# First unit's gates loaded on their own in sixteen rows, and another order of loads, scans and copies ahead of the first score

## The chip, the cores and the metric

The kernel runs on one core of a Trainium2 chip. The metric is the device time of one execution in microseconds (us). Before the change its median over three runs is 1085.26 us (1085.22 to 1085.31). The core's engines work side by side, each through its own queue in program order, and wait for each other on semaphores: TensorE (PE: matmuls and transposes; PEld is its weight load), VectorE (DVE), ScalarE (ACT), GpSimd (POOL), and SyncE (SP), whose queue issues the transfers (DMA).

## The reference

Attention with a forget gate, then two expert layers. Only the attention matters here, and in it the gate `f`:

```python
scores = scale * np.matmul(q, k.transpose(0, 1, 3, 2))     # q, k: (2, 8, 576, 64)
log_f = np.log(np.clip(f, 0.0001, 1.0))                     # f: (2, 8, 576)
cum = np.cumsum(log_f, axis=-1)
decay = cum[:, :, :, None] - cum[:, :, None, :]
scores = np.where(causal, -1000000000.0, scores + decay)
...                                                         # softmax over the keys, times v
x = attn_out.transpose(0, 2, 1, 3).reshape(B * S, H * D)    # then both expert layers on x
```

So the score of query i and key j needs the running sum of log f at i and at j.

## The kernel before, in words

The work is one long program. Attention comes first (to about 205 us of the span), then the expert layers. In attention the queries of each batch are cut into tiles of 128 rows; a unit is one tile and two heads. A loop over half units (one head at a time) issues for each: the exponential of the half unit before, two score matmuls, some warm-up matmuls into an unused PSUM tile (`warm`), transposes and value matmuls of earlier units, and a piece of the preparation of the next tile.

fp32 operands are split in a high and a low part (`hl`: ACT casts the high part, DVE subtracts to get the low part), transposed on PE into PSUM (`pt`), and copied out ("evacuated") into `qa`, `qb` for the queries and `kt`, `kb` for the keys. A score takes two matmuls: `qa` by `kt`, then `qb` by `kb`. The tiles `qb` and `kb` carry, in their rows from 64 up, constants and the running sums of log f, so that the second matmul adds the decay as well. `f` is loaded as 16 rows (2 batches by 8 heads) of 576; it is clamped, its log is taken, a scan makes the running sum `cum`, and `chl` holds the high and the low part of `cum`. For tile 0 (the first 128 positions) four transfers put these rows into `kb` and `qb` directly from `chl`. For all other tiles `chl` is written to DRAM (`cd`) and read back from there (`cum_k`, `cum_q`).

Nothing is reordered by a scheduler: each engine runs its instructions in the order in which the code issues them. The change touches the stretch from the first load to the first score, and the first step of the loop:

- L100: the activation table is loaded first on ACT.
- L199 to L209: loads of `f`, of the first 128 rows of q and k by halves of the heads (`raw`), and of the next 128 rows (`early`), all on SP.
- L211 to L217: constants; the clamp of `f`; the identity `idr` for the transposes.
- L219 to L249 (`cumulate`): log, scan, high and low part of `cum`, and the transfers from them. It is called for the positions 0 to 128 (L249), and for 128 to 576 in two parts.
- L253 to L266: mask and constant rows, written by GpSimd (`k_rows` is L190).
- L686 on: the splits of tile 0's first heads (L354, L355), 12 warm-ups, the transposes (L361) and evacuations (L307 to L313) of the first four heads, 8 warm-ups, the loop. The list `first` holds what the first two steps of the loop do for the other four heads. In the same steps the loop splits tile 1's `early` rows into `big` (L317, L319, L321) and transposes them.

The evacuations are shared out by `pick`, which gives each to ACT or DVE by a running estimate of how long each is busy.

## Time and profile before

| | |
|---|---|
| median of three runs | 1085.26 us |
| the profiled execution | 1085.22 us |
| its span, first to last instruction | 1083.4 us |
| outside the span | 1.8 us |
| PE busy | 1076.9 us, 99% of the span |
| DVE busy | 840.0 us, 78% |
| ACT busy | 545.0 us, 50% |
| POOL busy | 57.0 us, 5% |

Times in a profile count from the start of the span. In a timeline a row is: start, duration, engine, line of the kernel, operation, what is written and read, the shape, the number of instructions merged into the row, and in brackets how long the engine had been idle before and who released it. An fp32 matmul of the program is two passes on PE and shows as two. Instructions of one engine overlap a little at their ends, so the distance from start to start is shorter than the duration. SPq rows are the queue that issues transfers; the row ends when the transfer is issued, not when it lands. The view of windows gives busy time, and the number of instructions, of each stretch; PEclk there is the granted TensorE clock as a share of full speed.

### The profile page before, as it was taken

Reading aid. Unit: us, or ns where it says so; the run is one execution under the profiler, and the core shown is the slowest. Engines: PE = TensorE matmul, PEld = TensorE weight load, DVE = VectorE, ACT = ScalarE, POOL = GpSimd, SP = SyncE. Lnnn points to the kernel's source line nnn. Section 1 sums busy time; section 2 is a strip of 40 time slices with the busy share of each in tenths; the row PEclk is TensorE's granted clock in tenths of the full one; section 3 lists DMA queues with packets and bytes.
Section 4 is the critical chain, followed back from the end, with each engine's and each line's share of the span. In section 5 each row is a group of like instructions: output and inputs, shape, how many; then the busy total and the mean of one; then the engine's idle time right before and its main releaser. Section 6 shows DMA issues by size and latency. Waiting matters only on the chain.

```text
span 1083.4 us, 18373 instructions
## 1 busy us (share of the span) xinstructions
PE 1076.9 (99%) x6844; PEld 963.7 (89%) x6844; DVE 840.0 (78%) x1897; ACT 545.0 (50%) x1295; POOL 57.0 (5%) x110
## 2 busy tenths in 40 slices
PE   9999999999999999999999999999999999999998
PEld 8787779998989899898988989899898989899997
DVE  7856647878797888977888787887976559788994
ACT  7867632454426243343524435253442458787881
POOL 6422310000000000000000000000000000000000
PEclk9999999999999999999999999999999999999999
DMA  6534202023241424425343342524322341161402
GB/s 147 153 82 114 65 21 78 1 98 114 92 146 63 148 83 146 136 89 156 110 144 106 109 147 98 160 84 146 127 95 81 128 155 43 64 205 59 166 1 88
DMA packets 103805, 114.98 MB, mean 106 GB/s; under 512 B 35236, under 2 KB 63860, under 8 KB 103716
## 3 DMA queue, kind: packets, MB, share of 16 engines
q1 hardware_dynamic: 103716, 113.81, 33.2%
q8 instruction: 54, 0.88, 0.3%
q14 instruction: 35, 0.29, 0.1%
HBM read 82.24 MB, written 27.07 MB: 101 GB/s over the span
## 4 chain that ended last, share of the span: by engine, by line
PE 97%; DVE 1%; ACT 0%; issue 0%; POOL 0%; DVEq 0%; ACTq 0%; POOLq 0%
PE bank L858 33%; PE bank L1268 29%; PE bank L1740 9%; PE bank L1650 4%; PE ph L828 3%; PE x L568 3%; PE spare L1650 2%; PE bank L1579 2%; PE pa L858 2%; PE pa L641 2%; PE ph L622 1%; PE sp L468 1%; PE pt L532 1%; PE pt L361 1%; PE wt L395 1%; PE sp L469 1%
## 5 line engine op out<-in xcount | busy, mean ns | idle before, releaser
L858 PE MATMUL bank<-w2h,big 128*128 128x512 f32 x924 | 296.7, 390 | 0.0
L858 PE MATMUL bank<-w2l,big 128*128 128x512 f32 x528 | 205.7, 390 | 0.0
L858 PEld LDWEIGHTS bank<-w2h,big 128*128 128x128 f32 x924 | 173.4, 188 | 36.1 <-DVE hid_b L836 0.2
L1297 ACT COPY snap<-bank 128x288 f32<-128x288 f32 x168 | 66.8, 397 | 167.6 <-PE bank L1268 165.4
L835 ACT ACTIVATE big<-c 128x288 fp32r<-128x288 f32 x168 | 74.8, 445 | 84.7 <-DVE c L1302 81.3
L858 PEld LDWEIGHTS bank<-w2l,big 128*128 128x128 f32 x528 | 99.1, 188 | 20.0
L836 DVE SCALAR_TENSOR_TENSOR big<-c,big 128x288 fp32r<-128x288 f32 x140 | 64.0, 457 | 56.6 <-ACT big L835 53.9
L1033 DVE SCALAR_TENSOR_TENSOR acc<-bank,P,acc 128x512 f32<-128x512 f32 x132 | 92.2, 744 | 14.9 <-PE bank L858 14.8
L1268 PE MATMUL bank<-tt,ss 128*128 128x288 f32 x672 | 102.8, 295 | 0.0
L1268 PE MATMUL bank<-xh,ss 128*128 128x288 f32 x448 | 102.7, 295 | 0.0
L1268 PEld LDWEIGHTS bank<-tt,ss 128*128 128x128 f32 x672 | 93.1, 188 | 0.1
L1302 DVE TENSOR_TENSOR c<-bank,snap 128x288 f32<-128x288 f32 x168 | 75.7, 450 | 18.8 <-PE bank L1268 18.6
L1014 ACT CAST hb<-da 128x512 fp32r<-128x512 f32 x38 | 23.7, 623 | 106.8 <-DVE da L989 95.9
L1268 PEld LDWEIGHTS bank<-xh,ss 128*128 128x128 f32 x448 | 76.3, 188 | 0.0
L1268 PE MATMUL bank<-xl,ss 128*128 128x288 f32 x224 | 66.1, 295 | 0.0
L1268 PE MATMUL bank<-xh,w1l 128*128 128x288 f32 x224 | 66.0, 295 | 0.0
L1268 PE MATMUL bank<-xl,w1h 128*128 128x288 f32 x224 | 65.9, 294 | 0.0
L1268 PE MATMUL bank<-xh,w1h 128*128 128x288 f32 x224 | 65.7, 293 | 0.0
L858 PE MATMUL bank<-w2h,hid_b 128*128 128x512 f32 x132 | 51.4, 389 | 0.0
L75 DVE TENSOR_TENSOR w2l<-stg,w2h 128x512 fp32r<-128x512 f32 x60 | 41.2, 689 | 13.0 <-ACT w2h L74 12.9
L512 POOL TENSOR_SCALAR p<-p,rs 128x256 f32<-128x256 f32 (+5 forms) x72 | 41.8, 592 | 91.2 <-DVE rs L508 52.2
L1268 PE MATMUL bank<-tt,w1h 128*128 128x288 f32 x224 | 46.0, 293 | 0.0
(313 smaller groups left out, 2446.3 us busy)
## 6 DMA issues: line engine op xcount, KB each, us to landing
stg<-in_moe_w_dram SPq DMA_DIRECT2D x64, 512.0 KB
wb<-w_in_b SPq DMA_DIRECT2D x42, 256.0 KB
raw<-in_moe_w_in_dram SPq DMA_DIRECT2D x16, 512.0 KB
raw<-in_moe_w_out_dram SPq DMA_DIRECT2D x16, 512.0 KB
w_in_b<-hb SPq DMA_DIRECT2D x18, 256.0 KB
w_out_h<-hb SPq DMA_DIRECT2D x16, 256.0 KB
w_out_l<-da SPq DMA_DIRECT2D x16, 256.0 KB
w_in_f<-da SPq DMA_DIRECT2D x12, 256.0 KB
```

Source lines behind the costliest of these rows:

```text
L75: (lo_engine or nc.vector).tensor_tensor(out=lo, in0=raw, in1=f(hi), op=ALU.subtract)
L512: nc.gpsimd.tensor_scalar(out=p[:n, a, :nk], in0=p[:n, a, :nk], scalar1=r[:n, a:a + 1], scalar2=1.0, op0=ALU.mult, op1=ALU.mult,)
L568: nc.tensor.matmul(out=x[64 * a:64 * a + 64, h // 2, :n], lhsT=vts[b, j][:w, h + a, :], rhs=pT[:w, 128 * j + 64 * a:128 * j + 64 * a + 64] ...
L835: nc.scalar.activation(out=hh, in_=ph, func=AF.Relu)
L836: nc.vector.scalar_tensor_tensor(out=hl, in0=ph, scalar=0.0, in1=f(hh), op0=ALU.max, op1=ALU.subtract)
L858: nc.tensor.matmul(out=pa, lhsT=a_[:, ts_], rhs=w[wn][ft_], start=(first and n == 0), stop=(last and n == 2),)
L1033: nc.vector.scalar_tensor_tensor(out=acc[t], in0=pa, scalar=P[:, t, e:e + 1], in1=acc[t], op0=ALU.mult, op1=ALU.add)
L1268: nc.tensor.matmul(out=by_chunk(out_) if len(v_.shape) == 3 else out_, lhsT=u, rhs=v_, start=first and m == 0, stop=m == 5, skip_group_che ...
L1297: nc.scalar.copy(out=t, in_=bank["x", g])
L1302: nc.vector.tensor_tensor(out=t, in0=bank[of, g], in1=snap[with_, g], op=ALU.add)
L1650: nc.tensor.matmul(out=out_, lhsT=a_(kk, pa), rhs=b_(kk, pb), start=first and q == 0, stop=q == 5, skip_group_check=True,)
L1740: nc.tensor.matmul(out=bk[b][:, cs], lhsT=a_[:, ts_], rhs=w[wn][i][:, cs], start=i == 0 and q == 0, stop=i == 3 and q == 2,)
```

## The change

1. The gates of the first unit (batch 0, positions 0 to 128) are loaded on their own into `fe`, in sixteen rows: heads 0 to 3 twice, then heads 4 to 7 twice. Heads 0 to 3 come by SP's queue, heads 4 to 7 by ACT's; the activation table is loaded behind ACT's. DVE clamps `fe`, ACT takes the log, DVE scans it, and two DVE instructions turn each pair of copies into high and low part, in place by row: `part` and `sign`, made from the identity, are 0, 1 or -1 by row, so that a row becomes either the high part or what is left of it. One transfer per operand and half of the heads then fills both rows, four in all; the second two follow the loads of `early`.
2. The load of all of `f` comes behind the first halves of q and k. Its clamp runs on GpSimd ahead of the mask. Its log is taken in one piece (576 wide); the scan is cut at 256, one part before and one behind the evacuations of the first heads; high part (ACT) and low part (DVE) are made in one piece of 576, the low part behind the first score's reduction. The two direct transfers to `qb[1]` that followed `cd` are gone.
3. Of the first four heads ACT evacuates both query tiles and DVE both key tiles, instead of by `pick`; two of the 8 warm-ups stand between the query and the key transposes.

```diff
-    nc.scalar.preload_act_table_set("natural_log_exp_and_others")
...
                 out=t[:, 4 * g:4 * g + 4], in_=src[0, 4 * g:4 * g + 4, 0:128, :].rearrange("h p d -> p h d")
             )
 
-        nc.sync.dma_start(out=ft, in_=fg.rearrange("b h s -> (b h) s"))
+        fe, ce, me, he = (acc[0][:16, 128 * i:128 * i + 128] for i in range(4))
+        for g, queue in enumerate((nc.sync, nc.scalar)):
+            queue.dma_start(
+                out=fe[8 * g:8 * g + 8],
+                in_=fg[0, 4 * g:4 * g + 4, :128].unsqueeze(0).to_broadcast([2, 4, 128]),
+            )
+        nc.scalar.preload_act_table_set("natural_log_exp_and_others")
         for nm in "qk":
             raws[nm, 0, 0] = rawp.tile([128, H, D], F32, tag="raw", name="raw")
         for g in range(2):
             load_half(raws["q", 0, 0], q, g)
             load_half(raws["k", 0, 0], k, g)
+            if g == 0:
+                nc.sync.dma_start(out=ft, in_=fg.rearrange("b h s -> (b h) s"))
 
         early = stage.tile([128, 2, H, D], F32, tag="stg", name="early")
-        for a, (nm, src) in enumerate((("q", q), ("k", k))):
-            nc.sync.dma_start(out=early[:, a], in_=src[0, :, 128:256, :].rearrange("h p d -> p h d"))
-            raws[nm, 0, 128] = early[:, a]
+
+        def load_early():
+            for a, (nm, src) in enumerate((("q", q), ("k", k))):
+                nc.sync.dma_start(out=early[:, a], in_=src[0, :, 128:256, :].rearrange("h p d -> p h d"))
+                raws[nm, 0, 128] = early[:, a]
 
         nc.vector.memset(zer, 0.0)
         make_identity(nc, idn)
         k_rows(256, 384, nc.vector)
         q_rows(0, nc.gpsimd)
         q_rows(1, nc.gpsimd)
-        nc.vector.tensor_scalar(out=ft, in0=ft, scalar1=1e-4, scalar2=1.0, op0=ALU.max, op1=ALU.min)
+        nc.gpsimd.tensor_scalar(out=ft, in0=ft, scalar1=1e-4, scalar2=1.0, op0=ALU.max, op1=ALU.min)
+        part = acc[1][:16, :2]
+        sign = acc[1][:16, 8:9]
+        nc.vector.tensor_reduce(
+            out=part, in_=idn[:16, :16].rearrange("p (g a h) -> p a g h", g=2, a=2), axis=AX.XY, op=ALU.add
+        )
+        nc.vector.tensor_tensor(out=sign, in0=part[:, 0:1], in1=part[:, 1:2], op=ALU.subtract)
         nc.vector.tensor_copy(out=idr, in_=idn)
-
-        def cumulate(lo, hi, part=None):
-            w = hi - lo
-            if part != 1:
-                cumulate_a(lo, hi, w)
-            if part != 0:
-                cumulate_b(lo, hi)
-
-        def cumulate_a(lo, hi, w):
-            nc.scalar.activation(out=ft[:, lo:hi], in_=ft[:, lo:hi], func=AF.Ln)
+        nc.vector.tensor_scalar(out=fe, in0=fe, scalar1=1e-4, scalar2=1.0, op0=ALU.max, op1=ALU.min)
+        nc.scalar.activation(out=fe, in_=fe, func=AF.Ln)
+
+        def scan(o, i, init):
             nc.vector.tensor_tensor_scan(
-                out=cum[:, lo:hi], data0=ft[:, lo:hi], data1=zer.to_broadcast([16, w]),
-                initial=cum[:, lo - 1:lo] if lo else 0.0, op0=ALU.add, op1=ALU.add,
+                out=o, data0=i, data1=zer.to_broadcast([16, i.shape[1]]), initial=init, op0=ALU.add, op1=ALU.add,
             )
 
-        def cumulate_b(lo, hi):
-            nc.scalar.copy(out=chl[:, 0, lo:hi].bitcast(FR), in_=cum[:, lo:hi])
-            nc.vector.tensor_tensor(
-                out=chl[:, 1, lo:hi].bitcast(FR), in0=cum[:, lo:hi], in1=chl[:, 0, lo:hi], op=ALU.subtract
+        scan(ce, fe, 0.0)
+        nc.vector.tensor_scalar(out=me.bitcast(FR), in0=ce, scalar1=sign, scalar2=None, op0=ALU.mult)
+        nc.vector.scalar_tensor_tensor(
+            out=he.bitcast(FR), in0=ce, scalar=part[:, 1:2], in1=me, op0=ALU.mult, op1=ALU.add
+        )
+
+        def early_k(g):
+            nc.sync.dma_start(
+                out=f(kb[66:68, 4 * g:4 * g + 4, kbase[0]:kbase[0] + 128]), in_=he[8 * g:8 * g + 8]
             )
-            if lo == 0:
-                for a in range(2):
-                    nc.sync.dma_start(
-                        out=f(kb[66 + a:67 + a, :, kbase[0]:kbase[0] + hi]), in_=chl[:H, a, :hi]
-                    )
-                    nc.sync.dma_start(out=f(qb[0][64 + a:65 + a, :, :hi]), in_=chl[:4, a, :hi])
-                return
+
+        def early_q(g):
+            nc.sync.dma_start(out=f(qb[g][64:66, :, :128]), in_=he[8 * g:8 * g + 8])
+
+        early_k(0)
+        early_q(0)
+        load_early()
+        early_k(1)
+        early_q(1)
+
+        def long_rows():
+            nc.scalar.copy(out=chl[:, 0].bitcast(FR), in_=cum)
+            yield
+            nc.vector.tensor_tensor(out=chl[:, 1].bitcast(FR), in0=cum, in1=chl[:, 0], op=ALU.subtract)
             nc.sync.dma_start(out=cd.rearrange("a p s -> p a s"), in_=chl)
-            for a in range(2):
-                nc.sync.dma_start(out=f(qb[1][64 + a:65 + a, :, :lo]), in_=chl[4:8, a, :lo])
-
-        cumulate(0, 128)
+            cum_k(0, 128, 256)
+            yield
+
         load_v(0, 0)
         load_raw("q", q, 0, *QT[0][2])
         nc.sync.dma_start(out=wg, in_=w_gate.rearrange("(k p) e -> p k e", p=128))
             busy[e] += cost[e]
             return e
 
-        def evac(o, i, cols, scale=None):
-            if pick(act=90 + 0.83 * cols, dve=90 + 1.05 * cols) == "act":
+        def evac(o, i, cols, scale=None, by=None):
+            cost = dict(act=90 + 0.83 * cols, dve=90 + 1.05 * cols)
+            if pick(**({by: cost[by]} if by in cost else cost)) == "act":
                 if scale:
                     nc.scalar.activation(out=o, in_=i, func=AF.Copy, scale=scale)
                 else:
                     if n == 64:
                         evac(quads(a_)[:, :, 0:4:3], pv.rearrange("p (u z) t -> p u z t", z=2), 4 * n, 0.125)
                     else:
-                        evac(a_[:, :, :n], pv, 4 * n, 0.125)
+                        evac(a_[:, :, :n], pv, 4 * n, 0.125, early)
                     if early:
-                        evac(b_[0:64, :, :n], pv[0:64], 4 * n, 0.125)
+                        evac(b_[0:64, :, :n], pv[0:64], 4 * n, 0.125, early)
                     else:
                         duplicate(b_[0:64], a_[0:64])
                         if g:
                             cum_q(b, i, g, slots[g])
                 else:
                     o = kbase[b] + s0
-                    evac(kt[:, hs, o:o + n], pv, 4 * n)
+                    evac(kt[:, hs, o:o + n], pv, 4 * n, by=early)
                     if early:
-                        evac(kb[0:64, hs, o:o + n], pv[64:128], 4 * n)
+                        evac(kb[0:64, hs, o:o + n], pv[64:128], 4 * n, by=early)
                     else:
                         duplicate(kb[0:64, hs, o:o + n], kt[64:128, hs, o:o + n])
 
         (qs0, qt0), (ks0, kt0) = make_preps(0)
         qs0(0)
         ks0(0)
-        cumulate(128, S, 0)
+        nc.scalar.activation(out=ft, in_=ft, func=AF.Ln)
+        scan(cum[:, :256], ft[:, :256], 0.0)
         warm(12)
-        qt0(0, True)
-        kt0(0, True)
-        warm(8)
-        cumulate(128, S, 1)
-        cum_k(0, 128, 256)
+        qt0(0, "act")
+        warm(2)
+        kt0(0, "dve")
+        warm(6)
+        scan(cum[:, 256:], ft[:, 256:], cum[:, 255:256])
+        rows_ = long_rows()
+        next(rows_)
 
         first = [
-            lambda: (qs0(1), ks0(1), load_raw("k", k, 0, *KTL[2])), lambda: (qt0(1, True), kt0(1, True)),
+            lambda: (next(rows_), qs0(1), ks0(1), load_raw("k", k, 0, *KTL[2])),
+            lambda: (qt0(1, True), kt0(1, True)),
         ]
```

How the instructions now stand. On DVE, from the scan between the first splits to the first subtraction on `early`, before (`cum_136` holds f and `cum`, `cum_137` is `chl`, `pt` is PSUM, L355 the low parts of the other four heads; ISA rows are the reduction of a score and its read-out):

```order
L228 SCALAR_TENSOR_TENSOR cum_136<-cum_136,zer 16x448
L311 TENSOR_SCALAR qb_155<-pt 64x512
L313 CAST kb<-pt 64x4x128
L235 TENSOR_TENSOR cum_137<-cum_136,cum_137 16x448
L481 ISA p,nmax<-sp,mask 128x128
L481 ISA nmax 128x1
L355 TENSOR_TENSOR hl<-raw,hl 128x4x64 x2
L321 TENSOR_TENSOR big<-early,big 128x8x64
```

and after (`cum_135` holds f and `cum`, `cum_136` is `chl`; L375 and L341 are L355 and L321 of before):

```order
L237 SCALAR_TENSOR_TENSOR cum_135<-cum_135,zer 16x256
L333 CAST kt<-pt 128x4x128
L333 CAST kb<-pt 64x4x128
L237 SCALAR_TENSOR_TENSOR cum_135<-cum_135,zer 16x320
L501 ISA p,nmax<-sp,mask 128x128
L501 ISA nmax 128x1
L264 TENSOR_TENSOR cum_136<-cum_135,cum_136 16x576
L375 TENSOR_TENSOR hl<-raw,hl 128x4x64 x2
L341 TENSOR_TENSOR big<-early,big 128x8x64
```

Between the evacuations of the first heads and the splits of the other four heads there stood a subtraction of 448 and the first reduction; now there stand a scan of 320, the reduction, and a subtraction of 576.

On ACT, from the log of the first gates to the cast of `early`, before (`qa` and `qb` are the query tiles):

```order
L227 ACTIVATE cum_136<-cum_136 16x128
L234 CAST cum_137<-cum_136 16x128
L354 CAST hl<-raw 128x4x64 x2
L227 ACTIVATE cum_136<-cum_136 16x448
L307 ACTIVATE qa_152<-pt 128x512
L309 CAST kt<-pt 128x4x128
L234 CAST cum_137<-cum_136 16x448
L354 CAST hl<-raw 128x4x64 x2
L317 CAST big<-early 128x8x64
```

and after (`acc_94` holds the first unit's gates):

```order
L234 ACTIVATE acc_94<-acc_94 16x128
L374 CAST hl<-raw 128x4x64 x2
L709 ACTIVATE cum_135<-cum_135 16x576
L327 ACTIVATE qa_151<-pt 128x512
L327 ACTIVATE qb_154<-pt 64x512
L262 CAST cum_136<-cum_135 16x576
L374 CAST hl<-raw 128x4x64 x2
L337 CAST big<-early 128x8x64
```

The copy of the high part is now 576 wide and still stands ahead of the casts for the other four heads.

On POOL, from the last constant rows of `qb` for the first unit to the next constant rows of `qb`, before:

```order
L187 MEMSET qb_156 4x512
L253 MEMSET mask 128x704
L254 AFFINE_SELECT mask<-mask 128x704
L260 COPY mask_143<-mask 64x64 x2
L190 MEMSET kb 32x8x128
L186 MEMSET qb_157 32x512
```

and after:

```order
L186 MEMSET qb_155 4x512
L225 TENSOR_SCALAR cum_135<-cum_135 16x576
L272 MEMSET mask 128x704
L273 AFFINE_SELECT mask<-mask 128x704
L279 COPY mask_142<-mask 64x64 x2
L189 MEMSET kb 32x8x128
L185 MEMSET qb_156 32x512
```

The clamp of the whole of `f` (L225) stands ahead of the mask and of all the constant rows behind it, whose order stays.

## Rows read from the trace of the kernel before

**Rows 1.** The page: shares of the chain that ended last, by engine.

```profile
PE 97%; DVE 1%; ACT 0%; issue 0%; POOL 0%; DVEq 0%; ACTq 0%; POOLq 0%
```

**Rows 2.** Windows, PE: stretch, us, busy (count), PEclk, DMA share, GB/s.

```profile
1.39:5.82 4.43, 4.43 (x21) 1.00 0.76 174
5.82:8.65 2.83, 2.83 (x28) 1.00 0.51 116
...
12.77:13.61 0.84, 0.00 (x1) 1.00 0.18 45
```

**Rows 3.** The chain of waits: start us, us, what.

```profile
6.43 0.31 PE pt L361 x4
...
11.74 1.01 DVE big L319
```

**Rows 4.** Timeline of DVE, 2.5 to 13.5 us.

```profile
2.55 0.72 DVE L216 TENSOR_SCALAR cum<-cum 16x576 f32<-16x576 f32 x1 [0.54 <-DMA cum<-in_f_dram]
...
3.64 0.41 DVE L228 TENSOR_TENSOR_SCAN cum<-cum,zer 16x128 f32<-16x128 f32 x1 [0.25 <-ACT cum L227]
...
4.72 1.38 DVE L355 TENSOR_TENSOR hl<-raw,hl 128x256 fp32r<-128x256 f32 x2
...
6.02 1.13 DVE L228 TENSOR_TENSOR_SCAN cum<-cum,zer 16x448 f32<-16x448 f32 x1
...
8.11 0.69 DVE L313 CAST kb<-pt 64x512 fp32r<-64x512 f32 x1
...
8.72 0.60 DVE L235 TENSOR_TENSOR cum<-cum,cum 16x448 fp32r<-16x448 f32 x1
...
9.57 0.75 DVE L355 TENSOR_TENSOR hl<-raw,hl 128x256 fp32r<-128x256 f32 x2
...
11.66 1.08 DVE L319 CAST big<-early 128x512 fp32r<-128x512 f32 x1
...
12.77 0.69 DVE L321 TENSOR_TENSOR big<-early,big 128x512 fp32r<-128x512 f32 x1
```

**Rows 5.** Timeline of ACT.

```profile
3.30 0.31 ACT L227 ACTIVATE cum<-cum 16x128 f32<-16x128 f32 x1 [1.29 <-DVE cum L216]
...
4.09 0.30 ACT L234 CAST cum<-cum 16x128 fp32r<-16x128 f32 x1 [0.48 <-DVE cum L228]
...
7.72 0.56 ACT L234 CAST cum<-cum 16x448 fp32r<-16x448 f32 x1
```

**Rows 6.** Timeline of POOL.

```profile
3.92 0.69 POOL L253 MEMSET mask<- 128x704 f32 x1
...
8.47 3.98 POOL L190 MEMSET kb<- 32x2560 f32 x2
```

**Rows 7.** Groups by form, POOL, first 60 us; busy us, mean ns, idle before.

```profile
L512 POOL TENSOR_SCALAR p<-p,rs 128x512 f32<-128x512 f32 x8 | 5.5, 696 | 9.3 <-DVE rs L508 7.6 <-PE pt L361 1.8
```

**Rows 8.** Instructions on tile raw: ns min/median/max, first and last start.

```profile
L319 DVE CAST hl<-raw x1: 421/421/421, 19.3 to 19.3; 128x512 fp32r<-128x512 f32 x1
```

**Rows 9.** Timeline of SP's queue.

```profile
0.74 0.40 SPq L199 DMA_DIRECT2D cum<-in_f_dram  x1
...
2.20 0.51 SPq L195 DMA_DIRECT2D raw<-in_q_dram  x1
...
9.72 0.45 SPq L245 DMA_DIRECT2D cd<-cum  x1
...
11.96 0.26 SPq L271 DMA_DIRECT2D kb<-cd  x1
```

**Rows 10.** Timeline of PE.

```profile
9.71 0.66 PE L395 MATMUL wt<-idn 128*128 128x128 f32 x4
...
13.61 0.51 PE L361 MATMUL pt<-idr,big 128*128 128x128 f32 x4 [0.84 <-DVE big L321]
...
14.20 0.66 PE L395 MATMUL wt<-idn 128*128 128x128 f32 x4
...
18.51 0.28 PE L469 MATMUL sp<-kb,qb 96*128 96x256 f32 x1
```

## The prediction

> **What bounds the kernel now.** I read the page first, then the windows, the chain of waits, and the timeline of each engine from the first load to 19 us. On the page the chain that ends last runs through TensorE for 97% of the span [rows 1]. So a change pays or costs only where the chain leaves TensorE, or where TensorE itself gets more or fewer instructions. The edits all lie in the first 14 us. There the chain goes from the 12 warm-ups to the first transposes at 6.43, then over ScalarE and VectorE, and is on VectorE's cast L319 at 11.74 [rows 3]. TensorE stands still from 12.77 to 13.61, 0.84 us, until VectorE's subtraction L321 is done [rows 2, 10]. Behind that, by the share of 97%, it is on TensorE nearly all the time. What counts, then, is how late VectorE gets to L321 in the changed order: what is gained before that and lost again does not show at the end, and what is lost there goes through to the end one for one, since the later program is the same, instruction by instruction.
>
> **Up to the first transposes: nothing.** TensorE is busy with its 12 warm-ups from 1.39 to 6.43 and they stay. The first unit's gates come in two small transfers. The load of f was issued at 0.74 and VectorE started on it at 2.55, 1.81 us later [rows 4, 9]. The same from 0.74 gives 2.55 again; the half on ScalarE's queue is a thing the trace does not show, and I bound it by 1.81 and by the longest small transfer in the rows, 2.24 (`cd` issued at 9.72, read back at 11.96) [rows 9]. Then come a clamp, a log of 0.31, a scan of 0.41 [rows 4, 5], and two products and sums on 128 columns, which I take at no more than the scan: 2.55 + 0.41 + 0.31 + 0.41 + 2 x 0.41 + 0.1 for four hand-overs is 4.6. The low parts of the first heads' q and k took 1.38 us from 4.72, to 6.10 [rows 4]; from 4.6 they end no later. The activation table's load moves behind one issue on ScalarE; it began at once before, the log only at 3.30 [rows 5], and that distance covers it. All this is covered by the warm-ups; it costs something only if ScalarE's transfer is late by more than about 1 us. The four transfers of running sums to `kb` and `qb` now leave SP from about 4.6; two instead of four are needed by the first score, some 4 us later, against the 2.24 of a small transfer.
>
> **First score: 0 to 0.1 us.** The number of warm-ups and transposes on TensorE is the same. Two warm-ups, four passes of 0.10 each (28 passes in 2.83 us [rows 2]), now delay the key transposes: 6.43 + 0.31 + 0.40 + 0.31 is 7.45. VectorE then evacuates `kt` and `kb` itself, 0.61 apart (8.11 to 8.72 [rows 4]): `kb` starts at about 8.1, as it did before, when it waited behind `qb`. So the parallel evacuation gives no earlier first score; it is free for VectorE's next instruction at 8.72 to 8.8, before 8.72.
>
> **VectorE from there: 1.4 us later.** Before, a subtraction of 448 (0.60), the first reduction, and then at 9.57 the low parts of the other four heads [rows 4]. Now there stands a scan of 320. By the scans of 128 (0.41) and 448 (1.13) it takes 0.41 + 0.72 x 192/320 = 0.84: 8.75 to 9.6. Before, the scan of 448 ran from 6.02 beside the warm-ups, where nobody waited. The copy of the high part on ScalarE waits for this scan; by 0.30 for 128 and 0.56 for 448 [rows 5] it takes 0.67 for 576: 9.63 to 10.3. The casts for the other four heads are queued behind it on ScalarE, and the subtraction of 576 waits for it on VectorE, with the low parts of the other four heads behind it. The subtraction, 0.60 for 448, is 0.6 to 0.77 for 576; I take 0.73: 10.33 to 11.06, and the next starts 0.08 before its end, at 10.98. Against 9.57 that is 1.41 later. From there to the cast L319 the order is the same and took 11.66 - 9.57 = 2.09, so L319 would start at 13.07.
>
> **The cast beside GpSimd: 0.1 us given back, and 0.7 at most.** L319 took 1.08 us at 11.66, while the same form took 0.42 at 19.3 [rows 4, 8]. Beside it GpSimd's two fills of `kb` ran from 8.47 to 12.45 [rows 6]; the cast ended at 12.74, 0.29 after them. So it stood still until the fill was done. If the fills ended where they did, the cast would now take 0.42 and end at 13.49, only 0.75 later than before. But GpSimd is later too. Its queue gets the clamp of all of f ahead of the mask, which waits for that load. The load is now the fourth on SP, where the second half of q was issued at 2.20 [rows 9]; with 1.81 to 2.24 it lands at 4.0 to 4.45, behind the rows of q and k, and I take 4.3. The clamp of 576 columns on GpSimd is not in the trace; 512 columns of the same operation take 0.70 [rows 7], so 0.70 to 0.79. It ends at about 5.05, and the mask starts at 5.1 instead of 3.92 [rows 6]: 1.2 later (0.85 to 1.75, with 0.4 for a wait beside VectorE's splits at the upper end). The fills then end at 13.65, across the cast's start at 13.07, and the cast ends 0.29 later, at 13.94: 1.2 later than before.
> The Trainium skill, "SBUF — State Buffer", section "Who interferes with whom", says that such a VectorE cast and a GpSimd instruction exclude each other for a whole instruction, the later one standing still. By that rule the cast ends at 13.94; by mere sharing it would take 1.08 us again and end at 14.15, 1.4 later. The row of before, an end 0.29 behind the fill's, speaks for the rule.
> Ends for this term: 0.75 (no fill beside it) and 1.75. I take 1.3, between 1.2 and 1.4.
>
> **What is late next.** ScalarE's evacuations and the exponentials wait for the same VectorE instructions and shift with them. `cd` is written about 1.35 later, and what SP issues behind it shifts by as much; tile 1's second matmul, at 18.51 [rows 10], shifts by 1.3 too, so no new wait there. The two direct transfers to `qb[1]` that are gone freed SP where it now waits for `cd`. Sum: 1085.22 for the profiled execution (span 1083.4 and 1.8 around it) plus 1.3 is 1086.5; the median of the runs is 0.04 above that execution, which I leave out.
>
> **Rivals.**
> 1. *TensorE's clock falls (slower).* The granted clock reads 1.00 throughout [rows 2], yet the first 21 passes took 4.43 us, 0.21 each, and later ones 0.10: the first at the level of 1.2 GHz, the later at 2.4. After the still stand of 0.84 us the next warm-ups took 0.66 for four passes, as before it [rows 10]: no fall. Now there would be two such gaps: about 1.1 us ahead of the other heads' transposes (the second head's warm-ups end at 9.71 + 0.66 = 10.4 [rows 10], the first low part at 10.98 plus half of 0.75, and TensorE follows at about 11.5), and one at L321. If this makes the clock fall, a stretch like the first costs again 4.43 - 21 x 0.10 = 2.3 us: 1086.5 + 2.3 = 1088.8. It decides if the gap of 1.1 us is enough, which no row shows. The Trainium skill, "TensorE: Matmul & The Clock Gate", section "What's actually happening", says that the clock goes back to 1.2 GHz once the engine has been idle; the trace has the gap of 0.84 us without a fall.
> 2. *VectorE's order doesn't bind (faster).* If the scan and the copies are much shorter than I take, or start earlier, and L319 runs free of the fills, the wait of 0.84 us at L321 can go and no more, because TensorE is busy around it: 1085.2 - 0.8 = 1084.4. For it: the first scores' operands come earlier. Against it: 0.84 + 0.67 + 0.73 us stand in one chain behind `kb`.
> 3. *GpSimd gets later than I take.* If the load of f lands near 5, or the clamp and the mask wait for VectorE's scan, the fills end 2 us later or more and hold the cast as long: 1087.4.
> 4. *It is hidden.* If later waits with slack take up the shift, 1085.3. Against it: the chain has hardly any other engine in it after 13.61.
>
> **How the numbers follow.** Forecast (0.75 to 1.75 later, 1086.0 to 1087.0): 0.60. Rival 1: 0.09. Rival 2: 0.12. Rival 3: 0.11. Rival 4: 0.08. 0.2%, about what a measurement of this kernel can tell from no change, is 2.17 us: within it lies 1083.1 to 1087.4. Faster by more needs more than rival 2 can give; I leave 0.04. Slower by more: rival 1, half of rival 3, and 0.04 of the forecast's tail: 0.18. The rest, 0.78, is no change. The range runs from 1084.9 (half of rival 2 left out) to 1087.9 (rival 1 and the end of rival 3 left out).
>
> **What would show it.** In the profile after: the first reduction at about 9.6; the 576-wide subtraction starting at 10.3 behind a wait for ScalarE; the low parts of the other heads at about 11.0; the cast of `early` ending just behind GpSimd's last fill, near 13.9; TensorE's long wait ending near 14.9. It is wrong if the copy or the subtraction runs without that wait, if the fills end by 12.5, or if the passes behind the gaps take 0.21 again.

## The result, and the profile after

| | before | after |
|---|---|---|
| median, six runs each | 1085.24 us | 1091.13 us |
| lowest to highest | 1085.14 to 1085.31 | 1089.58 to 1092.54 |
| the profiled execution | 1085.22 us | 1089.58 us |
| its span | 1083.4 us | 1087.8 us |
| PE busy | 1076.9 us | 1079.5 us |

The change made the kernel slower: the ratio is 1.0054 [1.0044, 1.0064], 5.9 us. The forecast was 1086.5 us and the range ended at 1087.9, so both missed. The runs now lie up to 3 us apart, where they lay 0.2 apart before, and the profiled execution is the shortest of them.

The page after, clock by slices and chain by engine; it answers to [rows 1]:

```profile
PEclk8999999999999999999999999999999999999999
...
PE 97%; DVE 1%; POOL 1%; issue 0%; ACT 0%; DMA 0%; SPq 0%; DVEq 0%; POOLq 0%; ACTq 0%
```

GpSimd, which had 0% of the chain, now has 1% of it, and the first slice no longer has the full clock. The timeline of GpSimd after, against [rows 6]:

```profile
5.09 2.65 POOL L225 TENSOR_SCALAR cum<-cum 16x576 f32<-16x576 f32 x1 [1.56 <-DMA cum<-in_f_dram]
7.79 0.69 POOL L272 MEMSET mask<- 128x704 f32 x1
...
12.58 3.97 POOL L189 MEMSET kb<- 32x2560 f32 x2
```

The clamp of f is the first row: it starts at 5.09 and takes 2.65 us. The mask begins at 7.79 instead of 3.92, and the two fills end at 16.55 instead of 12.45, 4.10 later. ScalarE after, against [rows 5]:

```profile
7.77 0.68 ACT L709 ACTIVATE cum<-cum 16x576 f32<-16x576 f32 x1 [2.67 <-POOL cum L225]
8.36 0.57 ACT L327 ACTIVATE qa<-pt 128x512 fp32r<-128x512 f32 x1
...
11.29 0.67 ACT L262 CAST cum<-cum 16x576 fp32r<-16x576 f32 x1 [1.88 <-DVE cum L237]
```

The log of f stands in ScalarE's queue ahead of the evacuations, and it waited 2.67 us for GpSimd's clamp; `qa` follows at 8.36, 6.76 before. VectorE after, against [rows 4]:

```profile
5.01 0.74 DVE L375 TENSOR_TENSOR hl<-raw,hl 128x256 fp32r<-128x256 f32 x2
8.48 0.68 DVE L237 TENSOR_TENSOR_SCAN cum<-cum,zer 16x256 f32<-16x256 f32 x1 [2.74 <-ACT cum L709]
9.09 0.65 DVE L333 CAST kt<-pt 128x512 fp32r<-128x512 f32 x1
9.78 0.69 DVE L333 CAST kb<-pt 64x512 fp32r<-64x512 f32 x1
10.39 0.86 DVE L237 TENSOR_TENSOR_SCAN cum<-cum,zer 16x320 f32<-16x320 f32 x1
...
11.99 0.75 DVE L264 TENSOR_TENSOR cum<-cum,cum 16x576 fp32r<-16x576 f32 x1 [0.41 <-ACT cum L262]
12.67 0.74 DVE L375 TENSOR_TENSOR hl<-raw,hl 128x256 fp32r<-128x256 f32 x2
...
15.03 1.81 DVE L339 CAST big<-early 128x512 fp32r<-128x512 f32 x1
```

Down this list the delay grows in four steps. `kb` is evacuated at 9.78 instead of 8.11: 1.67. The low parts of the other heads start at 12.67 instead of 9.57: 3.10, of which 1.43 is the new order of the long rows. The cast of `early` starts at 15.03 instead of 11.66: 3.37. It ends at 16.84 instead of 12.74: 4.10, and that end lies 0.29 behind GpSimd's last fill (16.55), as it did before. TensorE after, against [rows 10]:

```profile
9.89 0.30 PE L488 MATMUL sp<-kt,qa 128*128 128x128 f32 x1 [1.60 <-DVE kt L333]
10.68 0.30 PE L489 MATMUL sp<-kb,qb 96*128 96x128 f32 x1 [0.49 <-DVE kb L333]
...
13.13 1.25 PE L381 MATMUL pt<-idr,hl 128*128 128x128 f32 x8 [0.31 <-DVE hl L375]
...
14.63 1.16 PE L415 MATMUL wt<-idn 128*128 128x128 f32 x4
...
17.71 0.64 PE L381 MATMUL pt<-idr,big 128*128 128x128 f32 x4
```

TensorE stood still for 1.60 us, then for 0.49; four warm-up passes take 1.16 us where they took 0.66. Windows of PE after (stretch, us, busy and count, PEclk, DMA share, GB/s), against [rows 2]:

```profile
8.65:11.29 2.64, 0.91 (x7) 1.00 0.92 209
11.29:18.11 6.82, 6.46 (x36) 0.50 0.49 99
```

From 11.29 to 18.11 the granted clock is 0.50, the level of 1.2 GHz; TensorE had been busy for 0.91 of the 2.64 us ahead of it.

### The profile page after: what moved, and what is told of

Read it like the earlier page. It is cut to its first block, busy times and chain, and to the rows that moved or that the text cites. A ratio compares the mean times of both kernels' runs of the same rounds, so it can differ in the third digit from the quotient of the medians.

```text
span 1087.8 us, 18375 instructions
## 1 busy us (share of the span) xinstructions
PE 1079.5 (99%) x6844; PEld 965.7 (89%) x6844; DVE 841.2 (77%) x1901; ACT 545.3 (50%) x1294; POOL 59.5 (5%) x111
## 4 chain that ended last, share of the span: by engine, by line
PE 97%; DVE 1%; POOL 1%; issue 0%; ACT 0%; DMA 0%; SPq 0%; DVEq 0%; POOLq 0%; ACTq 0%
PE bank L882 33%; PE bank L1292 29%; PE bank L1764 9%; PE bank L1674 4%; PE ph L852 3%; PE x L588 3%; PE spare L1674 2%; PE bank L1603 2%; PE pa L882 2%; PE pa L661 2%; PE ph L642 1%; PE sp L488 1%; PE pt L381 1%; PE pt L552 1%; PE sp L489 1%; PE sp L436 1%
```

## The experiments

The question is how much of the 5.9 us belongs to the length of GpSimd's clamp, to the clock, and to VectorE's long rows with the cast held behind the fills. The explanation at first was that the clamp is a slow operation on GpSimd and takes the other engines with it; the rival was that the clock does most of it. Where a run has the multiplication, the clamp is left out, so that values beyond its limits stay as they are.

As a ruler serves one instruction that every kernel has, the value matmul which waits for `pT` near 37 us; it lies behind everything that the change touches. In the timelines of TensorE of before and after:

```profile
36.87 0.88 PE L568 MATMUL x<-pT,v 128*64 128x128 f32 x12 [0.34 <-DVE pT L313]
```

```profile
41.08 0.88 PE L588 MATMUL x<-pT,v 128*64 128x128 f32 x12 [0.61 <-DVE pT L333]
```

It is 4.21 later after, and the spans differ by 4.4. So nearly all of the profiled loss is made before 37 us. All kernels that were timed several times (e7 and e9 ran once), with the place of this instruction in each profile ("full" means that every run had a mean granted clock of 0.999 or 1.0):

| kernel | median us | ratio to before | clock in its runs | that matmul, against 36.87 |
|---|---|---|---|---|
| after | 1091.13 | 1.0054 [1.0044, 1.0064] | fell in all | +4.21 |
| e1, clamp on VectorE | 1090.04 | 1.0038 [1.0024, 1.0053] | fell in all | +4.67 |
| e2, multiplication on GpSimd | 1088.50 | 1.0027 [1.0017, 1.0037] | fell in 5 of 8 | +3.51 |
| e3, warm-ups ahead of the first score | 1090.75 | 1.0050 [1.0035, 1.0065] | fell in 2 of 4 | +7.05 |
| e4, log behind the evacuations | 1089.34 | 1.0036 [1.0023, 1.0049] | fell in all | +3.55 |
| e10, warm-ups in all gaps | 1089.23 | 1.0036 [1.0022, 1.0050] | full | +4.09 |
| e11, e2 with warm-ups in all gaps | 1087.69 | 1.0022 [1.0013, 1.0031] | full | +2.05 |
| e14, e11 with both fills moved | 1088.46 | 1.0029 [1.0018, 1.0039] | full | +2.82 |
| e15, e11 with one fill moved | 1087.16 | 1.0019 [1.0009, 1.0028] | full | +1.29 |
| e13, before without 8 warm-ups | 1087.89 | 1.0022 [1.0013, 1.0031] | fell in all | +2.00 |
| e6, before with fills moved | 1084.92 | 0.9997 [0.9988, 1.0005] | full | -0.59 |

**e7: what the clamp costs on GpSimd alone.** Added to before, at the end of attention:

```diff
+        for _ in range(3):
+            for rows_n in (16, 128):
+                s_ = mask[:rows_n, :S]
+                nc.gpsimd.tensor_scalar(out=s_, in0=s_, scalar1=1e-4, scalar2=1.0, op0=ALU.max, op1=ALU.min)
+                nc.gpsimd.tensor_scalar(out=s_, in0=s_, scalar1=1.0, scalar2=1.0, op0=ALU.mult, op1=ALU.mult)
+                nc.gpsimd.tensor_scalar(out=s_, in0=s_, scalar1=1.0, scalar2=None, op0=ALU.min)
```

> The kernel before, and at the end of attention, on the mask that nobody reads any more, three times on GpSimd alone in a row and with nothing else to do: the clamp (maximum, then minimum), two multiplications, and a single minimum, 576 columns wide, on 16 and on 128 partitions. What is read is each one's duration; the kernel's own time is not of interest. Theory O (the operation itself is slow on GpSimd): the clamp takes 2.2 to 2.7 us on 16 partitions wherever it stands, the multiplications 0.75 to 0.80; a single minimum lies between, 1.1 to 1.4, if each comparison costs as much. Theory W (the clamp was long in the changed kernel because it was held beside VectorE's splits): it takes 0.75 to 0.80 here, as the multiplications do. 128 partitions take as long as 16 by both.

Groups by form, POOL, 140 to 180 us; busy us, mean ns of one, idle before:

```profile
L796 POOL TENSOR_SCALAR mask<-mask 16x576 f32<-16x576 f32 x3 | 6.4, 2129 | 0.3
L798 POOL TENSOR_SCALAR mask<-mask 128x576 f32<-128x576 f32 x3 | 5.0, 1655 | 0.2
L798 POOL TENSOR_SCALAR mask<-mask 16x576 f32<-16x576 f32 x3 | 4.9, 1646 | 0.2
...
L797 POOL TENSOR_SCALAR mask<-mask 16x576 f32<-16x576 f32 x3 | 2.0, 662 | 0.3
```

The operation decides: 2.13 us for the clamp, 0.66 for an instruction of the same shape with two multiplications, 1.65 for a minimum alone (the expectation had 1.1 to 1.4), and the number of partitions does not count. In the changed kernel the clamp took 2.65, so 2.13 of it is its own. The other 0.5 came from what ran beside it, likely VectorE's low parts (5.01 to 5.75); in e9, where the clamp starts at 5.79, it takes 2.12 again.

**e2: the clamp's length in the kernel.**

```diff
-        nc.gpsimd.tensor_scalar(out=ft, in0=ft, scalar1=1e-4, scalar2=1.0, op0=ALU.max, op1=ALU.min)
+        nc.gpsimd.tensor_scalar(out=ft, in0=ft, scalar1=1.0, scalar2=1.0, op0=ALU.mult, op1=ALU.mult)
```

> The changed kernel with the clamp of all of f on GpSimd replaced by a multiplication by one with the same shape (the clamp of the long rows is left out). Tells whether the 2.65 us are the operation's. If maximum and minimum are what is slow on GpSimd: 0.7 to 0.8 us, the fills end near 14.6, the cast is held until 14.9, and the time is 1086.8 to 1087.6. If it is the shape (16 partitions, 576 columns) or a wait beside VectorE: 2 to 2.65 us again and 1089 or more.

GpSimd's timeline:

```profile
5.16 0.79 POOL L225 TENSOR_SCALAR cum<-cum 16x576 f32<-16x576 f32 x1 [1.63 <-DMA cum<-in_f_dram]
...
10.54 3.97 POOL L189 MEMSET kb<- 32x2560 f32 x2
```

It takes 0.79, and the fills end at 14.51 instead of 16.55, two microseconds earlier, as expected. The kernel is still slower than before, and the median (1088.50) lies above the expected 1087.6. Of its runs, the three at full clock took 1087.43 to 1087.76, the five in which the clock fell 1088.05 to 1089.2.

**e1: the clamp on VectorE**, behind the first low parts.

```diff
-        nc.gpsimd.tensor_scalar(out=ft, in0=ft, scalar1=1e-4, scalar2=1.0, op0=ALU.max, op1=ALU.min)
...
+        nc.vector.tensor_scalar(out=ft, in0=ft, scalar1=1e-4, scalar2=1.0, op0=ALU.max, op1=ALU.min)
         nc.scalar.activation(out=ft, in_=ft, func=AF.Ln)
```

> The changed kernel with the clamp of all of f on VectorE, behind the low parts of the first heads, instead of on GpSimd. Theory P (the clamp of 2.65 us on GpSimd pushes everything behind it late: the log on ScalarE, the scan on VectorE, and the fills of kb that hold the cast of early): the clamp takes under 0.4 us from about 5.8, qa is evacuated at once, the fills end near 12.5 again, the cast of early is free at about 13.7 and TensorE's long wait ends 0.8 to 1.2 later than in the kernel before: 1085.8 to 1086.6. Theory Q (the long chain of scan, copy and subtraction behind kb is the main loss, about 1.4): 1086.5 to 1087. Theory C (TensorE's clock falls because the new order leaves gaps, whatever GpSimd does): still 1088 or more, with runs that differ by 1 us or more.

VectorE's timeline:

```profile
6.16 1.83 DVE L708 TENSOR_SCALAR cum<-cum 16x576 f32<-16x576 f32 x1
...
15.30 0.42 DVE L338 CAST big<-early 128x512 fp32r<-128x512 f32 x1
```

Freeing GpSimd did what it should for the fills: they ended at 12.80 and the cast took 0.42. But the clamp itself, 0.72 at [rows 4], now took 1.83 beside GpSimd's copies and fills, the low parts of the other heads came at 12.93, and the clock fell. By its time only the expectation built on the clock held. The edit does not separate the two causes.

**e4: the log behind the evacuations**, with one scan of 576.

```diff
-        nc.scalar.activation(out=ft, in_=ft, func=AF.Ln)
-        scan(cum[:, :256], ft[:, :256], 0.0)
...
-        scan(cum[:, 256:], ft[:, 256:], cum[:, 255:256])
+        nc.scalar.activation(out=ft, in_=ft, func=AF.Ln)
+        scan(cum, ft, 0.0)
```

> The changed kernel with the log of all of f and its scan, now in one piece of 576, behind the evacuations of the first heads, so that nothing ahead of the first score waits for GpSimd's clamp. Theory Q (the queues behind that log are what costs): first score at about 8.9, the low parts of the other heads at about 11.5, 1087 to 1087.6. Theory P: the first score is early, but the fills still end at 16.5 and hold the cast of early until 16.8, so TensorE's long wait ends at about 17.3 as before and the time is 1088.8 or more; with TensorE standing still for longer, the clock may fall all the same.

Timelines of TensorE, GpSimd and VectorE:

```profile
8.61 0.30 PE L489 MATMUL sp<-kb,qb 96*128 96x128 f32 x1 [0.19 <-issue]
...
12.07 1.25 PE L381 MATMUL pt<-idr,hl 128*128 128x128 f32 x8 [1.99 <-DVE hl L375]
```

```profile
12.78 4.25 POOL L189 MEMSET kb<- 32x2560 f32 x2
```

```profile
13.97 1.32 DVE L339 CAST big<-early 128x512 fp32r<-128x512 f32 x1
```

The first score's second matmul starts at 8.61 instead of 10.68: the log ahead of the evacuations is what held it. That is worth little at the end. The scan of 576 and its copies now stand where all of it is in VectorE's way, TensorE stands still for 1.99 us ahead of the other heads, and the clock falls there. Of the two times only that of theory P held, and of its reasons only the clock: the fills end late (17.03), but the cast did not wait for that. It began inside the first fill, which takes 2.23 us and so ended at 15.01, and was done at 15.29; the second fill then took longer (4.25 for both, 3.97 in after). So the cast can get through between the two fills, and what it loses depends on when it begins.

**e3 and e10: the clock.** e3 has 14 warm-ups instead of 6 ahead of the first score; e10 has, besides, more in the loop's first steps:

```diff
-        warm(6)
+        warm(14)
...
-                warm((2,2,2,2,2,2,2,2,1,1,1,1,1,1,1,1)[s])
+                warm((2,4,2,10,2,2,2,2,1,1,1,1,1,1,1,1)[s])
```

> The changed kernel with 14 warm-ups instead of 6 ahead of the first score, which fill the gap in which TensorE stood still (8.3 to 9.9). Theory C: the granted clock stays at 1.00, the runs agree within 0.3 us and the time falls by 3 us or more, to 1088 or less. Theory P: the clock stays at 1.00 and the runs agree, but the cast of early is still held by the fills until 16.8, so 1088.8 to 1089.6. If eight more warm-ups are not enough, the clock falls as before and the runs still differ.

> The changed kernel with warm-ups in all places in which TensorE stands still for long: 14 ahead of the first score, 4 in the second step of the loop, 10 in the fourth. If the spread of the runs and the rest of the loss over 4 us are TensorE's clock (theory C), the granted clock is 1.00 in every run, the runs agree within 0.4 us, and the time is that of the GpSimd chain alone (theory P): the cast of early ends at 16.84 instead of 12.74, so 1085.3 + 4.1 = 1089.4 (1089.0 to 1089.9). If filling the gaps doesn't hold the clock, the runs spread from 1089 to 1092.5 as before.

In e3 the wait of 1.60 us is filled, and the one at the cast takes its place. TensorE's timeline and windows of e3:

```profile
17.71 0.72 PE L381 MATMUL pt<-idr,big 128*128 128x128 f32 x4 [1.87 <-DVE big L341]
```

```profile
10.00:17.48 7.48, 5.40 (x49) 1.00 0.57 119
17.48:24.30 6.82, 6.59 (x35) 0.50 0.41 102
```

The clock falls at 17.48, and the matmul at 37 us is 7.05 late. In e10 with that gap filled too, the clock stays full in all runs and it is 4.09 late. The difference, 2.96, is what a fall at this point cost. e10's median is 1.9 below that of after, and its runs lie 0.4 apart instead of 3. What the clock had added to the median is then about 1.9, a difference of two medians without an interval of its own; 3.9 stay without it, against the median of 1085.33 that the kernel before had beside e10.

**e13: the clock by itself**, on the kernel before.

```diff
-                warm((2,2,2,2,2,2,2,2,1,1,1,1,1,1,1,1)[s])
+                warm((0,0,0,0,2,2,2,2,1,1,1,1,1,1,1,1)[s])
```

> The kernel before, without the 8 warm-ups of the first four steps of the loop and with nothing else changed: TensorE stands still about 1.7 us longer between 9 and 13.6, and the chain over VectorE is the same. Theory C: the granted clock falls to 0.5 for some 7 us in some or all runs, and the time rises by 1 to 3 us with runs that differ. If gaps of this size do not make the clock fall: 1085.0 to 1085.4, or less where the warm-ups stood in TensorE's way.

Timeline and windows of TensorE:

```profile
10.30 0.93 PE L361 MATMUL pt<-idr,hl 128*128 128x128 f32 x8 [0.63 <-DVE hl L355]
...
13.61 0.72 PE L361 MATMUL pt<-idr,big 128*128 128x128 f32 x4 [1.12 <-DVE big L321]
```

```profile
8.65:11.30 2.65, 1.52 (x13) 1.00 0.86 194
11.30:18.10 6.80, 5.68 (x33) 0.50 0.49 116
```

VectorE's last subtraction ahead of these transposes and GpSimd's fills are where they were, and the transposes start at 13.61 as before. Yet the matmul at 37 us is 2.00 late and the kernel 1.0022 [1.0013, 1.0031] slower. Taking work away from TensorE made the program longer, and up to 37 us the clock is what differs. In this profile another 1.6 us are added between 500 and 600 us, at full clock; TensorE waits there at 518.00 and 524.25, for 0.28 and 0.21 us, which is too little, and why is not settled.

**e9: both halves of the first gates on one queue.**

```diff
-        for g, queue in enumerate((nc.sync, nc.scalar)):
+        for g, queue in enumerate((nc.sync, nc.sync)):
```

> The changed kernel with both halves of the first gates on SP's queue. Theory Q (two queues that issue at once hold each other, which is why they took 0.83 and 1.24 us and f's clamp began at 5.09): each takes 0.40 to 0.55 here, the first q is issued at 1.7 to 1.8 as before or 0.1 later, the clamp on GpSimd starts at 5.0 to 5.3, so nothing was lost by it. Theory B (the form of the transfer, the same rows read twice, is what makes the issue long): each takes 0.8 or more, q is issued at 2.4 or later and the clamp starts at 5.7 or later. By both the first score is no earlier than 10.6, and the time 1089.5 to 1092.5.

Timelines of the transfer queues, after (SP and ACT) and e9 (SP):

```profile
0.74 0.83 SPq L200 DMA_DIRECT2D acc<-in_f_dram  x1
...
2.81 0.50 SPq L211 DMA_DIRECT2D cum<-in_f_dram  x1
```

```profile
0.73 1.24 ACTq L200 DMA_DIRECT2D acc<-in_f_dram  x1
```

```profile
0.74 1.58 SPq L200 DMA_DIRECT2D acc<-in_f_dram  x2
...
3.35 0.50 SPq L211 DMA_DIRECT2D cum<-in_f_dram  x1
```

GpSimd's timeline of e9:

```profile
5.79 2.12 POOL L225 TENSOR_SCALAR cum<-cum 16x576 f32<-16x576 f32 x1 [2.27 <-DMA cum<-in_f_dram]
```

On one queue each half still takes 0.79 to issue, twice the 0.40 of [rows 9], so two queues did not cause it, though ScalarE's 1.24 is more than either. It is the form of this transfer that is long; that reading the rows twice makes it so is likely, but no run changes that alone. All of f leaves SP 0.54 later and GpSimd's clamp starts at 5.79 instead of 5.09, but takes 2.12 instead of 2.65. The one run took 1089.57, as the profiled run of after.

**e11, e14, e15: what is left without the clamp's length and without a fall of the clock.** All have the multiplication of e2 and more warm-ups (the first two edits below). e14 moves the fills of `kb` as well, as shown. e15 leaves `k_rows(512, 832)` where it is, moves only the pieces of the other fill, and has 3 warm-ups instead of 7 in the fourth step:

```diff
-        warm(6)
+        warm(8)
-                warm((2,2,2,2,2,2,2,2,1,1,1,1,1,1,1,1)[s])
+                warm((3,7,2,7,2,2,2,2,1,1,1,1,1,1,1,1)[s])
-        k_rows(512, 832)
-        k_rows(0, 256)
-        late_rows = [lambda: None] * 5 + [lambda: cum_k(0, 256, S)]
+        late_rows = [lambda: None] + [lambda c=c: k_rows(c, c + 80) for c in range(512, 832, 80)] + [lambda: cum_k(0, 256, S)]
+        late_rows += [lambda c=c: k_rows(c, c + 64) for c in range(0, 256, 64)]
```

> The changed kernel with the multiplication in the place of GpSimd's clamp (the clamp of the long rows is left out), and with warm-ups in the places where TensorE stands still. The prediction's own sum, with the load of f landing at 5.1 instead of 4.3 and no fall of the clock: the fills end at 14.5, the cast at 14.8, 2.05 later than before: 1087.3 (1086.9 to 1087.8), with runs that agree within 0.4 us. If more than the clamp and the clock was missing from that sum, 1088 or more.

> The changed kernel with the multiplication by 1 on GpSimd in place of the clamp (the clamp is left out), the additional warm-ups that keep TensorE from standing still, and GpSimd's two big fills of kb cut in small pieces and moved behind the first score, into later steps. Chain theory (VectorE's long rows cost 1.4 us, the rest of the loss is the cast held by the fills): the cast of early starts at about 13.5 and takes 0.42, TensorE's transposes of it start at 14.8 to 14.9 instead of 15.68, and the time is 1086.4 to 1087.1. Rival (the fills don't matter; whatever runs beside the cast holds it): 1087.5 to 1088.0, as with the fills.

> The changed kernel with the multiplication by 1 on GpSimd in place of the clamp (the clamp is left out) and additional warm-ups, of which three, not seven, stand at the cast; of GpSimd's two big fills of kb only the one for batch 1 is moved behind the first scores, so that the one for batch 0 still runs at 10.5 to 12.6, ahead of the cast. Chain theory (the long rows' 1.4 us remain, the fills' hold is gone): the cast of early starts at 13.5 to 13.7 and takes 0.42, TensorE's transposes of it start at 14.8 to 15.0 (13.61 before the change, 15.68 with both fills in place), no wait for a transfer to kb near 30, and the time is 1086.4 to 1087.0. Rival (a shift that is repaired here is lost behind it again, as with both fills moved): 1087.5 to 1088.5.

e11 came as expected: the cast, begun at 13.56 beside the fills, takes 1.25. e14 did not. The cast took 0.42 and the subtraction began at 14.18, but seven warm-ups that filled the old gap now held the transposes until 15.73, and near 30 us TensorE waited for a copy into `kb`. TensorE's timeline of e14:

```profile
14.20 1.78 PE L414 MATMUL wt<-idn 128*128 128x128 f32 x14
15.73 0.54 PE L380 MATMUL pt<-idr,big 128*128 128x128 f32 x4
...
30.42 0.42 PE L488 MATMUL sp<-kb,qb 96*128 96x384 f32 x1 [0.46 <-DMA kb<-kt]
```

The first is the edit's own. The copy was issued at 25.88, in e11 at 25.79, and landed at about 30.3; why it took so long is not settled. e15 has neither wait; VectorE's and TensorE's timelines:

```profile
8.63 0.69 DVE L333 CAST kb<-pt 64x512 fp32r<-64x512 f32 x1
...
11.52 0.74 DVE L375 TENSOR_TENSOR hl<-raw,hl 128x256 fp32r<-128x256 f32 x2
...
13.61 0.42 DVE L339 CAST big<-early 128x512 fp32r<-128x512 f32 x1
```

```profile
14.90 0.51 PE L381 MATMUL pt<-idr,big 128*128 128x128 f32 x4
```

The cast is free of the fills, and the transposes start at 14.90, 1.29 after the 13.61 of before; the shift stays 1.29 at 37 us. The place is as expected, the median (1087.16) 0.16 above the expected range: in the profile, 0.6 more is added between 500 and 1000 us.

The 1.29 is a sum of three. `kb` is evacuated at 8.63 instead of 8.11: 0.52. From there to the low parts of the other heads it takes 2.89 instead of 1.46, which is 1.43 for the long rows. And the cast, no longer beside a fill, takes 0.42 instead of the 1.08 that it takes in the kernel before: 0.66 given back.

So the loss without a fall of the clock comes apart, by the matmul near 37 us: 4.09 in e10; 2.05 in e11, so 2.04 belong to the clamp's length; 1.29 in e15, so 0.76 belong to the second fill's hold of the cast; and 1.29 are left. By the medians, each against the kernel before that was timed beside it, the three are 3.9, 2.4 and 2.0 us.

**e6: the hold of the cast, on the kernel before.** Both fills of `kb` in small pieces in later steps, as in e14.

> The kernel before, with the constant rows of kb from column 512 on and those of batch 1 filled in pieces, one in each later step of the loop, instead of in two fills ahead of the loop. The cast of early is then not held: it takes 0.42 instead of 1.08 and TensorE's wait at 12.77 shrinks by 0.66. If the hold is what GpSimd's order costs: 1084.6 (1084.4 to 1084.8), faster than both. If the pieces hold up GpSimd's normalization or other casts later: 1085.2 or more. If the cast is slow for another reason: 1085.3.

VectorE's and TensorE's timelines:

```profile
11.73 0.42 DVE L318 CAST big<-early 128x512 fp32r<-128x512 f32 x1
```

```profile
13.01 0.51 PE L360 MATMUL pt<-idr,big 128*128 128x128 f32 x4 [0.18 <-DVE big L320]
```

The cast takes 0.42 instead of 1.08, TensorE's wait shrinks from 0.84 to 0.18, and the transposes start 0.60 earlier: the hold is real in the kernel before, too. By the medians that is 0.4 us, less than the 0.5 to 0.9 that were expected; the interval holds 1, so it is not shown as a gain. No version is shown to beat the kernel before.

## Why the prediction was wrong, step by step

- **Up to the first transposes: nothing.** Right. The low parts were done at 5.75, earlier than the 6.10 of before. The activation table's load cost nothing.
- **First score, 0 to 0.1 us: wrong**, 10.68 for its second matmul. The term leaves out the log of 576 and the scan of 256, which now stand ahead of the evacuations. The prediction set the clamp's end at 5.05; it ended at 7.74. The log, with ScalarE's evacuations behind it, and the scan, with VectorE's of `kt` behind it, both waited for that; in e4, with both behind the evacuations, the second matmul starts at 8.61. The order costs something with a short instruction in the clamp's place, too: in e15 that ends at 6.00, the scan takes 1.27 (0.68 in after), and `kb` is 0.52 late. Why the scan is longer there is not shown.
- **VectorE's long rows, 1.41: right.** 1.43 in the profile: scan 0.86 (0.84 taken), copy 0.67 (0.67), subtraction 0.75 (0.73); 1.43 again in e15. That the whole shift is 1.29 there, the 1.3 of the forecast, is chance: the forecast has 1.41 less 0.1, and e15 has 0.52 and 1.43 less 0.66.
- **The cast beside GpSimd: the rule right, the term wrong.** The cast ended 0.29 behind the fill, as in the kernel before. So the rule of the Trainium skill, "SBUF — State Buffer", section "Who interferes with whom", on which the sum did not rest, agrees with 16.55 and 16.84; in e4 it is the fill that runs, the first, that the cast waits for. But the fills were to end at 13.65. The 2.90 us between are the step that failed: **the clamp of 576 columns, sized 0.70 to 0.79, took 2.65**, 1.9 more. The size was read from [rows 7], the same kind of instruction on the same engine, called "the same operation" without asking which arithmetic it does: that one multiplies, this one takes a maximum and a minimum. e7 shows 0.66 against 2.13, so 1.4 of the 1.9 is the arithmetic; the other 0.5 is likely a wait beside VectorE, for which the prediction had 0.4 at its upper end. Another 0.8 is the load of f, taken to land at 4.3, there at 5.09; 0.6 of it because it was issued at 2.81 and not at 2.20, mostly for the first gates' transfer, which is long to issue (e9). The rest, 0.2, is GpSimd's own work ahead of the fills.
- **Rival 1, the clock, 0.09: it came, and was given too little.** Its condition was a gap of about 1.1 us ahead of the other heads' transposes. There it was 0.31; the gaps of 1.60 and 0.49 came earlier, ahead of the first score, where the prediction had none. What spoke against it was that the gap of 0.84 in the kernel before was followed by no fall. e13, with gaps of 0.63 and less ahead of the fall, shows that the length of one gap alone does not tell. Its price, 2.3, lies within what the falls cost: 2.00 in e13, 1.46 in e2 (3.51 against the 2.05 of e11), 2.96 in e3. In the profiled run of after it is only 0.12 (4.21 against the 4.09 of e10), since TensorE would have waited for the cast anyhow. The other five runs of after have no profile; that their 0.8 to 3 us more come from falls at dearer moments fits e3, and is not shown.
- **Rival 3, GpSimd later than taken, 0.11: it came as well**, by the load near 5. Its price of 0.9 over the forecast was too small, since the fills were 4.1 late and not 2; no rival had a longer clamp.
- **The chances.** Rivals 1 and 3 were priced as if apart. Here they came together: a later GpSimd made TensorE stand still, and the clock fell behind that. The range would not have held without the clock either: e10, at full clock, takes 1089.2, and the range ended at 1087.9. With a multiplication in the clamp's place and full clock (e11) it is 1087.7, inside the range.

## What to carry to other kernels

Size an instruction by a row of the same arithmetic, not only of the same kind, shape and engine; where there is none, the upper end of the range is several times the nearest row. When work moves to an idle engine, list what is queued behind its consumers: one long operation on GpSimd held ScalarE's evacuations, VectorE's scan and its cast. Where a change makes TensorE wait more in a stretch that was already loose, add the price of a lower clock to the same case, not to a rival of its own; and measure with warm-ups in the gaps to tell the two apart.

## What was not expected of the hardware

- On GpSimd a maximum and a minimum over 576 columns take 2.13 us and a minimum alone 1.65, two multiplications in one instruction 0.66, for 16 and for 128 partitions alike (e7).
- A transfer that reads four rows twice took 0.79 to 0.83 us to issue on SP and 1.24 on ScalarE's queue; that of all 16 rows of f took 0.40 to 0.50.
- VectorE's cast, begun beside the first of GpSimd's two fills, ended 0.28 us behind that one and ahead of the second, and the two fills then took 4.25 us instead of 3.97 (e4).
- VectorE's clamp of 16 by 576 took 1.83 us beside GpSimd's copies and fills (e1), against 0.72 [rows 4].
- Eight warm-ups fewer made the program 2.6 us longer by the medians, with the same work on every other engine (e13); 2.0 of it is there by 37 us, with the fall of the clock.
